# Rolling the DMA issue loop and moving 16 KB of a weight per DMA engine in a memory-bound decode kernel

## The chip, the cores and the metric

One core of one Trainium2 chip. The metric is device time in microseconds of one execution, the median of several. The kernel before takes 660.9 us. All timed runs used here are in the fast state. Four kernels (e3, e4, e7, e8) ran once each, so their state is unknown; of these the landings and packets in the trace are used, and no fine difference of their times.

## The reference

One decode step of two parallel branches whose sum is added to x: attention over a long cache (2 batches, 32 heads, 8192 cached positions of 128), and a small feed-forward part.

```python
# x: [2, 1, 512], k_cache and v_cache: [2, 32, 8192, 128], all bfloat16
xn = layernorm(x)
q = (xn @ wq) per head                       # wq: 512 x 4096
p = softmax(q . k_cache * 128 ** -0.5)
a = (p . v_cache, heads joined) @ wo         # wo: 4096 x 512
b = relu(xn @ w1) @ w2                       # w1: 512 x 1792, w2: 1792 x 512
out = x + a + b
```

The two caches are 268 of the 280.5 MB that are read; everything else is small.

## The kernel before

The 64 heads (2 batches of 32) are taken two at a time, 32 pairs in all. K and V of a pair are loads of 4 MB each, into two buffers each. SyncE issues all of the loads but that of x, unrolled over the pairs; TensorE (PE), VectorE (DVE) and ScalarE (ACT) loop. (Shortened: `out_view` stands for the output, rearranged.)

```python
sp.dma_start(w1_sb, B_w1.rearrange("(p kt) f -> p kt f", kt=KT)).then_inc(dW1, 16)
sp.dma_start(w2_sb, B_w2.rearrange("(p j) n -> p j n", j=FT)).then_inc(dW2, 16)   # FT = 14
load_k(0)
load_k(1)
load_v(0)
for t in range(NP - 2):                  # NP = 32 pairs
    sp.wait_ge(pT[NG - 1], t + 1)        # PE has transposed all of the old K
    load_k(t + R)                        # R = 2
    sp.wait_ge(sW, t + 1)                # PE has used all of the old V
    load_v(t + 1)
# ... the last V in two halves, then wo in five pieces
sp.wait_ge(sE, 1)
sp.dma_start(out_view, osb[:]).then_inc(dO, 16)
```

The feed-forward part runs before the first pair, while K is being loaded (w2 has 14 rows on each partition, so 14 matmuls):

```python
for j in range(FT):                      # PE: h = xn @ w1, 128 columns at a time
    for kt in range(KT):
        pe.matmul(hp[:, j, :], lhsT=w1_v[:, kt, j, :], rhs=xz[:, kt, Z:Z + Bsz], ...)
v.tensor_scalar(out=hT[:], in0=hp, scalar1=0.0, scalar2=None, op0=ALU.max)
for j in range(FT):                      # PE: y = relu(h) @ w2
    pe.matmul(y, lhsT=hT[:, j, :], rhs=w2_sb[:, j, :], ...)
v.tensor_tensor(out=ys[:], in0=y, in1=xsb[:], op=ALU.add)
```

At the end `ys` is put into the accumulator `fin` by four f32 matmuls against a 2x2 identity, and the products with wo are added there as the pieces of wo arrive.

## Time and profile before

| | before |
|---|---|
| median of the three runs before the prediction (of all six: 660.90) | 660.88 us |
| span of the profiled run | 658.6 us |
| data moved | 280.66 MB |
| share of the 16 DMA engines' span that the data queue fills | 99.2% |
| last piece of wo lands | 654.85 us |

The span is read first by busy shares, then by stretches, then by waits and by the end of the chain; the lines stand in the prediction below. Beside them two kinds of records of the trace are used that no view prints. One is the semaphore updates of a load: the K and V loads have 16 each, and the page counts 16 DMA engines, so I read each as one engine's landing of its share, and their 16 times show how far the engines are apart. The other is the list of the DMA packets with their size, start and duration. I give both as plain numbers.

The 16 updates of four loads of the kernel before, as microseconds after the first of them:

```
K of pair 0  (first  31.01): 0 .08 .14 .17 .19 .19 .20 .23 .24 .24 .24 .25 .26 .37 .38 | 1.72
V of pair 0  (first  50.42): 0 .10 .13 .19 .21 .22 .23 .24 .26 .27 .28 .37 .38 | 1.72 1.78 1.82
V of pair 1  (first  69.85): 0 .10 .12 .20 .21 .22 .23 .24 .35 .36 | 1.69 1.72 1.73 1.75 1.78 1.83
K of pair 31 (first 623.57): 0 .04 .14 .15 .17 .20 .21 .36 .42 | 1.69 1.71 1.73 1.74 1.76 1.82 1.84
```

Engines become late one at a time and do not catch up: one late engine at first, three by V of pair 0, six by V of pair 1, seven at the end. An engine is called late here when it stands in the right group; the differences of up to 0.4 us within a group are called start offsets.

### The profile page before, as it was taken

The numbers are of one execution on the slowest core, as the hardware profiler recorded it, in microseconds if no ns is written. First come the engines' busy times: TensorE is split into PE (matmuls) and PEld (weight loads), VectorE is DVE, ScalarE is ACT, GpSimd is POOL, SyncE is SP. The second block draws the span as 40 slices with busy tenths as digits, with TensorE's granted clock in tenths as the row PEclk, the third lists the DMA queues.
The fourth block names the chain that finished last, engine by engine and source line by source line (L and its number), as shares of the span: only waits on it lengthen the run. The fifth ranks groups of instructions, "written<-read, shape, count | busy, mean of one in ns | idle before, by whom it ended". The sixth has DMA issues, their size and how long they took to land.

```text
span 658.6 us, 26859 instructions
## 1 busy us (share of the span) xinstructions
PE 559.9 (85%) x12737; PEld 535.1 (81%) x12737; DVE 253.2 (38%) x436; ACT 255.8 (39%) x403; POOL 9.0 (1%) x46
## 2 busy tenths in 40 slices
PE   2998799987989878879887887997878997887896
PEld 0488798987879878879887887987878987887895
DVE  1144344442434433334443343443434443333441
ACT  1043444443433434334353434344333444333340
POOL 1000000000000000000000000000000000000000
PEclk9799999998998988999898899898989998898988
DMA  8999999999999999999999999999999999999996
GB/s 365 430 444 418 439 430 429 432 428 442 422 442 424 436 428 432 432 428 444 420 442 428 432 430 430 434 430 442 424 436 428 432 432 428 440 424 442 426 424 281
DMA packets 10542, 280.66 MB, mean 426 GB/s; under 512 B 1186, under 2 KB 1188, under 8 KB 1700
## 3 DMA queue, kind: packets, MB, share of 16 engines
q1 hardware_dynamic: 10528, 280.50, 99.2%
q8 instruction: 9, 0.15, 0.1%
q14 instruction: 1, 0.01, 0.0%
q10 hardware_dynamic: 4, 0.00, 0.0%
HBM read 280.50 MB, written 0.00 MB: 426 GB/s over the span
## 4 chain that ended last, share of the span: by engine, by line
DMA 58%; PE 37%; ACT 2%; issue 1%; SPq 1%; ACTq 0%; DVE 0%
DMA ks<-in_A_k_cache_dram 54%; PE tp L285 21%; PE Sc L292 11%; PE ot L305 4%; DMA w_sb<-in_A_wo_dram 4%; ACT kT L412 2%; ACT L412 1%; SPq L187 0%; PE Sc L340 0%; SPq L182 0%; PE Sc L343 0%; SPq L170 0%; SPq L169 0%; SPq L163 0%; PE ot L397 0%
## 5 line engine op out<-in xcount | busy, mean ns | idle before, releaser
L285 PE MATMUL tp<-identb,ks 128*128 128x128 bf16 x4096 | 323.5, 229 | 68.4 <-DMA ks<-in_A_k_cache_dram 68.4
L412 DVE COPY kT<-tp 128x1024 bf16<-128x1024 bf16 x320 | 219.7, 691 | 324.3 <-PE tp L285 324.2
L285 PEld LDWEIGHTS tp<-identb,ks 128*128 128x128 bf16 x4096 | 254.8, 102 | 72.3 <-DMA ks<-in_A_k_cache_dram 72.2
L412 ACT COPY kT<-tp 128x1024 bf16<-128x1024 bf16 x192 | 194.3, 1012 | 233.4 <-PE tp L285 233.3
L292 PE MATMUL Sc<-q,kT 128*128 128x64 bf16 x4096 | 216.8, 196 | 7.6 <-ACT kT L412 5.7
L292 PEld LDWEIGHTS Sc<-q,kT 128*128 128x128 bf16 x4096 | 178.4, 100 | 11.3 <-ACT kT L412 9.0
L305 PE MATMUL ot<-prm,vs 128*128 128x64 bf16 x4224 | 156.1, 192 | 4.2 <-issue 4.2
L305 PEld LDWEIGHTS ot<-prm,vs 128*128 128x128 bf16 x4224 | 139.0, 97 | 7.0 <-issue 4.4
L525 ACT COPY nm<-Sc 128x2 f32<-128x2 f32 x32 | 5.1, 160 | 118.5 <-PE Sc L343 118.5
L529 ACT ACTIVATE prm<-Sc,nm 64x128 bf16<-64x128 f32 x64 | 25.7, 401 | 4.3
L466 DVE TENSOR_REDUCE mcol<-Sc 64x1 bf16<-64x128 f32 x64 | 18.6, 290 | 18.7 <-PE Sc L292 18.3
L412 ACT ACT_TABLE_LOAD x16 | 20.5, 1283 | 2.2
L240 PE MATMUL ot<-vs,xz 128*16 128x512 bf16 x32 | 9.5, 470 | 8.6 <-DMA vs<-in_A_wq_dram 8.6
L517 ACT COPY OTf<-ot 128x2 f32 x32 | 5.1, 160 | 26.9 <-PE ot L305 26.9
L471 DVE TENSOR_REDUCE mx<-Sc 1x2 bf16<-1x128 bf16 x32 | 8.9, 278 | 16.9 <-PE Sc L340 16.9
L240 PEld LDWEIGHTS ot<-vs,xz 128*16 128x16 bf16 x32 | 3.3, 105 | 14.4 <-issue 12.2
L225 POOL COPY q<-qb 128x2 bf16<-128x2 bf16 x32 | 5.8, 184 | 588.9 <-PE Sc L292 566.1
L529 ACT ACTIVATION_READ_ACCUMULATOR prm<-Sc,nm x64 | 11.8, 185 | 0.0
L442 DVE TENSOR_SCALAR qs<-ot 16x512 bf16<-16x512 f32 x1 | 0.7, 679 | 18.0 <-PE ot L240 18.0
L340 PE MATMUL Sc<-identb,mcol 128*1 128x128 bf16 x32 | 7.0, 217 | 0.0
L270 PE MATMUL Sc<-w_sb,hT 128*2 128x512 bf16 x14 | 5.8, 604 | 0.1
L343 PE MATMUL Sc<-mx,onesb 1*128 1x2 bf16 x32 | 5.5, 172 | 0.0
(56 smaller groups left out, 37.5 us busy)
## 6 DMA issues: line engine op xcount, KB each, us to landing
ks<-in_A_k_cache_dram SPq DMA_DIRECT2D x32, 4096.0 KB, 26.7
vs<-in_A_v_cache_dram SPq DMA_DIRECT2D x31, 4096.0 KB, 31.3
vs<-in_A_wq_dram SPq DMA_DIRECT2D x1, 4096.0 KB, 12.1
vs<-in_A_v_cache_dram SPq DMA_DIRECT2D x2, 2048.0 KB, 19.3
w_sb<-in_B_w_dram SPq DMA_DIRECT2D x2, 1792.0 KB, 17.9
w_sb<-in_A_wo_dram SPq DMA_DIRECT2D x1, 1792.0 KB, 25.4
w_sb<-in_A_wo_dram SPq DMA_DIRECT2D x1, 896.0 KB, 27.1
w_sb<-in_A_wo_dram SPq DMA_DIRECT2D x1, 768.0 KB, 28.5
```

The costliest lines, as they stand in the source:

```text
L225: g.tensor_copy(q2[t % R][:], qb[:, 2 * t:2 * t + 2]).then_inc(sQ1, 1)
L240: i = pe.matmul(qp, lhsT=xz[:, kt, Z - g * Bsz:Z - g * Bsz + QG * Bsz], rhs=vs[1][:, (kt * QG + g) * 512:(kt * QG + g + 1) * 512], start=( ...
L270: i = pe.matmul(y, lhsT=hT[:, j, :], rhs=w2_sb[:, j, :], start=(j == 0), stop=(j == FT - 1),)
L285: t = pe.transpose(tp[e % 4][:, i, :], ks[r][:, kk * Dh:(kk + 1) * Dh], identb[:])
L292: t = pe.matmul(Sc[r][:, 2 * kk:2 * kk + 2 * REP], lhsT=kT[e % 4][:, i, :], rhs=rep(q2[r][:]), start=True, stop=True,)
L305: t = pe.matmul(ot[r][:, 0:2 * REP], lhsT=vs[r][:, kk * Dh:(kk + 1) * Dh], rhs=rep(prm[r][:, kk, :]), start=(kk == 0), stop=(kk == KB - 1),)
L340: pe.transpose(tr_of(r), mcol[r][:], identb[:]).then_inc(sT, 1)
L343: pe.matmul(bc_of(r), lhsT=onesb[:], rhs=mx[r][:], start=True, stop=True).then_inc(sB, 1)
L412: fn(kT[e % 4][:], tp[e % 4][:]).then_inc(kR[e], 1)
L466: m = v.tensor_reduce(out=mcol[i][half, :], in_=S_of(i)[half, :, u], axis=AX.X, op=ALU.max)
L471: v.tensor_reduce(out=mx[i][:], in_=tr_of(i).rearrange("o (u m) -> o u m", u=2), axis=AX.X, op=ALU.max, negate=True,).then_inc(sX, 1)
L529: x = a.activation(out=prm[i][half, :, u], in_=S_of(i)[half, :, u], func=ACTF.Exp, bias=nm[i][half, u:u + 1], scale=1.0, accum_out=RS[half ...
```

## The change

It has three parts. SyncE's 60 steady loads become four in a loop of 15 passes, with addresses and wait values from registers. Of w2, 12 rows stay on each of the 128 partitions; the other 256 rows go to the lower 64 partitions, four on each, by eight loads of 8 partitions, meant to run on the same eight DMA engines; so these carry 16 KB more than before and the eight others 16 KB less. And at the end `ys` is transposed instead of multiplied, kept aside, and added in the last step. The intent of the second part seems to be to even out the DMA engines; it is called the shift below, and the third part the tail. The eight are called the low engines, 0 to 7, the others the high engines, 8 to 15. The trace numbers none: in the prediction this was an assumption, and the numbers of single low engines below are names for their places on the ladder of e7 (engine 7 has one extra row there, engine 6 two, and so on).

```diff
+    FA = FT - 2
+    FB = 2 * (FT - FA)
+    FJ = FA + FB
...
-        sp.dma_start(w2_sb, B_w2.rearrange("(p j) n -> p j n", j=FT)).then_inc(dW2, 16)
+        sp.dma_start(
+            w2_sb[:, 0:FA, :], B_w2[0:P * FA, :].rearrange("(p j) n -> p j n", j=FA)
+        ).then_inc(dW2, 16)
+
+        w2_v = B_w2[P * FA:, :].rearrange("(j p) n -> p j n", p=HP)
+        for p in (0, 1, 2, 3, 32, 33, 34, 35):
+            sl = slice(p, p + 29, 4)
+            sp.dma_start(w2_sb[sl, FA:FJ, :], w2_v[sl]).then_inc(dW2b, 16)
         load_k(0)
         load_k(1)
         load_v(0)
-        for t in range(NP - 2):
-            sp.wait_ge(pT[NG - 1], t + 1)
-            load_k(t + R)
-            sp.wait_ge(sW, t + 1)
-            load_v(t + 1)
+        reg = nc.alloc_register(mybir.EngineType.SP, "pairno_sp")
+        sp.reg_mov(reg, 0)
+        with sp.Fori(0, NP // R - 1) as tr:
+            for r in range(R):
+                sp.reg_add(reg, reg, 1)
+                sp.wait_ge(pT[NG - 1], reg)
+                sp.dma_start(
+                    ks[r][:], K_all[bass.ds(tr * (R * P) + (R + r) * P, P), :]
+                ).then_inc(dK[r], 16)
+                sp.wait_ge(sW, reg)
+                sp.dma_start(
+                    vs[1 - r][:], V_all[bass.ds(tr * (R * P) + (1 + r) * P, P), :]
+                ).then_inc(dV[1 - r], 16)
...
-        for j in range(FT):
+        for j in range(FJ):
+            half = slice(0, HP if j >= FA else P)
             i = pe.matmul(
                 y,
-                lhsT=hT[:, j, :],
-                rhs=w2_sb[:, j, :],
+                lhsT=hT[half, j, :],
+                rhs=w2_sb[half, j, :],
...
-            pe.matmul(
-                fin[:, k, :],
-                lhsT=ys[:, k * P:(k + 1) * P],
-                rhs=ident2[:],
-                start=(k == 0),
-                stop=False,
-            )
+            t = pe.transpose(yst[:, k, :], ys[:, k * P:(k + 1) * P], ident2[:])
+        t.then_inc(sH, 1)
...
-        v.tensor_scalar(
-            out=hT[:], in0=hp, scalar1=0.0, scalar2=None, op0=ALU.max,
-        ).then_inc(sF, 1)
+        for o, h in (
+            (hT[:, 0:FA, :], hp[:, 0:FA, :]),
+            (hT[0:HP, FA:FJ:2, :], hp[0:HP, FA:FT, :]),
+            (hT[0:HP, FA + 1:FJ:2, :], hp[HP:P, FA:FT, :]),
+        ):
+            t = v.tensor_scalar(out=o, in0=h, scalar1=0.0, scalar2=None, op0=ALU.max)
+        t.then_inc(sF, 1)
...
-        v.tensor_copy(yT[:], ot[0][:, 0:KT * Bsz].rearrange("p (b c) -> p b c", c=KT)).then_inc(sV, 1)
+        v.tensor_tensor(
+            out=yT[:],
+            in0=ot[0][:, 0:KT * Bsz].rearrange("p (b c) -> p b c", c=KT),
+            in1=xT[:].rearrange("p c b -> p b c"),
+            op=ALU.add,
+        ).then_inc(sV, 1)
```

(Cut: buffer sizes, the new semaphore, the w1 columns that go with the rows, and the counts of later waits.)

More of the change, by code (lines that the diff above doesn't have):

```diff
@@ L72 @@
     vs = [sb([P, SLOT], bf16, f"vs{i}") for i in range(R)]
-    w_sb = sb([P, max(WJ * D, KT * Dff + FT * D)], bf16, "w_sb")
+    w_sb = sb([P, max(WJ * D, KT * Dff + FJ * D)], bf16, "w_sb")
     w1_sb = w_sb[:, 0:KT * Dff].rearrange("p (kt f) -> p kt f", kt=KT)
-    w2_sb = w_sb[:, KT * Dff:KT * Dff + FT * D].rearrange("p (j n) -> p j n", j=FT)
+    w2_sb = w_sb[:, KT * Dff:KT * Dff + FJ * D].rearrange("p (j n) -> p j n", j=FJ)
     wo_sb = w_sb[:, 0:WJ * D].rearrange("p (j n) -> p j n", j=WJ)
@@ L106 @@
     OX = sb([P, WJ, Bsz], bf16, "OX")
-    hT = sb([P, FT, Bsz], bf16, "hT")
+    hT = sb([P, FJ, Bsz], bf16, "hT")
     ys = sb([Bsz, D], f32, "ys")
+    xT = sb([P, KT, Bsz], f32, "xT")
     yT = sb([P, Bsz, KT], bf16, "yT")
@@ L123, in bc_of @@
         return Sc[i][:, 480:482]
-    dX, dO, dW1, dW2 = sem("dX"), sem("dO"), sem("dW1"), sem("dW2")
+    dX, dO, dW1 = sem("dX"), sem("dO"), sem("dW1")
+    dW2, dW2b = sem("dW2"), sem("dW2b")
     dK = [sem(f"dK{i}") for i in range(R)]
@@ L153 @@
     y = Sc[1][0:Bsz, :]
+    yst = ot[0][:, 16:16 + KT * Bsz].rearrange("p (c b) -> p c b", c=KT)
     fin = ot[0][:, 0:KT * Bsz].rearrange("p (b c) -> p c b", c=KT)
@@ L248, in _ @@
         pe.wait_ge(dW1, 16)
-        w1_v = w1_sb.rearrange("p kt (f j) -> p kt j f", j=FT)
+        w1_a = w1_sb[:, :, 0:P * FA].rearrange("p kt (f j) -> p kt j f", j=FA)
         for j in range(FT):
@@ L254, in _ @@
                     hp[:, j, :],
-                    lhsT=w1_v[:, kt, j, :],
+                    lhsT=w1_a[:, kt, j, :] if j < FA else w1_sb[:, kt, j * P:(j + 1) * P],
                     rhs=xz[:, kt, Z:Z + Bsz],
@@ L268, in _ @@
         pe.wait_ge(dW2, 16)
-        for j in range(FT):
+        pe.wait_ge(dW2b, 16 * 8)
+        for j in range(FJ):
+            half = slice(0, HP if j >= FA else P)
             i = pe.matmul(
                 y,
-                lhsT=hT[:, j, :],
-                rhs=w2_sb[:, j, :],
+                lhsT=hT[half, j, :],
+                rhs=w2_sb[half, j, :],
                 start=(j == 0),
-                stop=(j == FT - 1),
+                stop=(j == FJ - 1),
             )
@@ L400, in _ @@
                         rhs=OX[:, j, :],
-                        start=False,
+                        start=(j == 0 and k == 0),
                         stop=(j == WJ - 1 and k == KT - 1),
@@ L490, in _ @@
         ).then_inc(sV, 1)
+        v.wait_ge(sH, 2)
+        v.tensor_copy(xT[:], yst)
         v.wait_ge(sW, NP + 1)
@@ L494, in _ @@
         ).then_inc(sV, 1)
-        v.wait_ge(sH, 2)
+        v.wait_ge(sH, 3)
         v.tensor_copy(Ob[:], tp[0][0:H, 0:Bsz, :]).then_inc(sV, 1)
-        v.wait_ge(sH, 3)
+        v.wait_ge(sH, 4)
         v.tensor_copy(
@@ L500, in _ @@
         ).then_inc(sV, 1)
-        v.wait_ge(sH, 4)
-        v.tensor_copy(yT[:], ot[0][:, 0:KT * Bsz].rearrange("p (b c) -> p b c", c=KT)).then_inc(sV, 1)
         v.wait_ge(sH, 5)
+        v.tensor_tensor(
[4 more added lines that the diff above has]
+        ).then_inc(sV, 1)
+        v.wait_ge(sH, 6)
         v.tensor_copy(osb[:], tp[1][0:Bsz * KT, 0, :]).then_inc(sE, 1)
```

## The prediction

> **What bounds the kernel now.** I read the page first: busy shares, slices and DMA queues.
>
> ```profile
> span 658.6 us, 26859 instructions
> PE 559.9 (85%) x12737; PEld 535.1 (81%) x12737; DVE 253.2 (38%) x436; ACT 255.8 (39%) x403; POOL 9.0 (1%) x46
> DMA  8999999999999999999999999999999999999996
> ...
> DMA packets 10542, 280.66 MB, mean 426 GB/s; under 512 B 1186, under 2 KB 1188, under 8 KB 1700
> ...
> q1 hardware_dynamic: 10528, 280.50, 99.2%
> q8 instruction: 9, 0.15, 0.1%
> ```
>
> No compute engine is full, and the 16 DMA engines are: the data queue q1 alone fills 99.2% of their span. Then the same by stretches (microseconds from the start; columns are length, then PE, PEld, DVE, ACT and POOL busy, granted clock, DMA share, GB/s):
>
> ```profile
> 0.00:33.00 33.00, 19.51 (x114) 8.94 (x115) 4.05 (x13) 2.94 (x4) 3.43 (x16) 0.90 0.95 398
> 150.00:600.00 450.00, 388.15 (x8971) 378.84 (x8968) 179.92 (x304) 182.26 (x288) 4.42 (x24) 0.94 1.00 432
> 600.00:640.00 40.00, 34.10 (x776) 33.49 (x773) 15.50 (x27) 15.88 (x25) 0.00 (x0) 0.91 1.00 429
> 640.00:658.60 18.60, 13.18 (x356) 11.94 (x353) 2.05 (x8) 1.23 (x6) 0.00 (x0) 0.85 0.73 303
> ```
>
> For 450 us the share is 1.00 at 432 GB/s: there is no hole to fill. Next, who waits: first the kernel's engines, then the DMA-issuing queue of SyncE.
>
> ```profile
> PE tp L285 <- DMA ks<-in_A_k_cache_dram: 68.4, 27, 3.4
> ```
>
> ```profile
> SPq L158 <- PE tp L285: 429.8, 30, 39.8
> SPq L161 <- PE ot L305: 148.6, 30, 8.2
> ```
>
> PE waits for K tiles 27 times; SyncE mostly sleeps until a buffer comes free, and is never short of time. Last, the end of the chain (start, length, what):
>
> ```profile
> 625.69 0.04 issue
> 625.73 29.12 DMA w_sb<-in_A_wo_dram
> 654.85 0.05 issue
> 654.90 0.39 PE ot L397 x8
> 655.29 0.02 issue
> 655.31 0.18 DVE yT L502
> 655.49 0.04 issue
> 655.53 0.28 PE tp L406
> 655.81 0.02 issue
> 655.84 0.21 DVE osb L504
> ```
>
> The last piece of wo lands at 654.85 and 3.8 us of small work follow. So the end is set by the moment at which the slowest DMA engine finishes its share of the queue.
>
> The trace's semaphore updates refine this, since each load posts one update per DMA engine. For K tile 0 (issued at 2.36) 15 updates come between 31.01 and 31.39 and one at 32.73. The number of late ones grows to seven by 110 us and stays: for the last K tile nine come at +0.00 to +0.42 us and seven at +1.69 to +1.84. The group means are 0.19 and 1.76, 1.57 apart. The last wo piece has eight early and eight late. The nine 16384-byte packets of q8 start at 29.57, 41.77, 47.79, 54.95, 61.06, 68.32, 107.20, 650.36 and 654.27: seven by 110, one more before the end, one after most data. So one instruction fetch makes one engine about 1.57 us late, for good, because its queue never runs dry. At the first fetch that is seen directly: the fetch holds an engine for 1.06 us and that engine's next 32 KB takes 1.681 instead of 1.213. The other engines' 32 KB packets stay at 1.213 meanwhile, so the limit is each engine's own rate (27 GB/s), not a shared one.
>
> [...] Against a fear of loops, PE, DVE and ACT already loop 16 times here and only one fetch falls between 70 and 650 us. [...] The trace gives no engine numbers; it shows 16 updates per load.
>
> **The change, part by part.**
>
> *w2.* Before, w2 is 14 rows of 1 KB on each partition; an engine has 8 packets of 14336 bytes, 535 ns each: 4.28 us. After, every partition takes 12 rows. A 12288-byte packet, interpolated between the 7168-byte (274) and 16384-byte (615) packets, is about 463 ns, so 8 take 3.70: minus 0.58 us on all engines. The other 256 rows go by eight loads of 8 partitions[...], to engines 0 to 7: 32 packets of 1 KB for each of these. The two 1 KB packets of x took 44 ns, so 1.41 us, plus seven more semaphore writes at 9 ns: 1.47. Net: engines 8 to 15 have 0.58 us less, engines 0 to 7 have 0.9 us more. Bytes are the same in total.
>
> This pays if the fetches sit on engines 8 to 15. I take that as the author's reason for picking the low engines; no number in the trace proves it. Then late engines, at most +1.84 now, come to about +1.26, and the early ones, at most +0.42, to about +1.32. The maximum falls from 1.84 to 1.32: **0.52 us off the last landing**, and off the time.
>
> *Rolled SyncE.* Sixty unrolled loads become four in a loop of 15 passes. Issues take 0.33 us each before[...]. A K load is issued 26.7 us before it lands and needs about 9.7 us of service (4.19 MB at 432 GB/s), so 17 us of lateness would be hidden. The shorter program may save a fetch[...] and seven late engines instead of eight leave the last one where it is. Effect: 0.
>
> *Start.* Eight more issues at about 0.46 us delay K tile 0's issue from 2.36 to about 6, with data queued until beyond 21 us: 0. The second feed-forward product has 16 matmuls instead of 14 at 0.43 (+0.85), the relu three small operations instead of one of 0.19 (about +0.35). It ended at 32.4, just before K tile 0 landed; now at about 33.6. PE begins its pairs about 1 us late, the load of K tile 2 is issued at 44.7 instead of 43.7, and V tile 0 keeps the engines busy to 50.4: 5.7 us of slack, so 0.
>
> *Tail.* Four f32 transposes replace matmuls that took 1.05 us at 643.59. They are off the path: PE has OX at 650.1 and then waits for wo. The copy of x for the later addition waits beside other work. The final yT gains an addend: 0.17 us becomes about 0.19. Effect: +0.02.
>
> Sum: 660.88 - 0.52 + 0.02 = **660.4 us**.
>
> **The rivals.** First, the fetches sit on low engines, or are spread over both halves. Then a low engine is at +1.84 + 0.9 = +2.74, and the time is 660.88 + 0.9 = 661.8. For it: the trace has no engine numbers. Against: the change would be senseless, and its 16 KB each way (0.6 us down, 0.9 up) splits a 1.57 us gap almost in half, which looks designed. I give it one in six.
>
> Second, the 1 KB packets cost much more than 44 ns each under load, say 70: then low engines gain 1.7 and the end is +2.1, 661.2. For it: 44 ns was seen on idle engines. Against: 2048-byte packets took 85 ns under full load, the same per byte.
>
> Third, the DMA limit is shared, so moving bytes between engines gives nothing: 660.9. Against: the constant 1.213 us beside the stalled engine.
>
> Fourth, the SyncE loop itself fetches at its branches, 15 times: spread over 8 engines, up to two each, 3 us more, 664. Against: the three loops that are there already do not.
>
> **Range and chances.** Runs of before spread over 0.2 us. The main case (about seven in ten) gives 660.0 to 660.8; rivals two and three end just above; so 659.9 to 661.3 should hold it 8 times in 10. A change of 2% is 13.2 us and nothing here is that large: within 2% 0.985, faster 0.005, slower 0.01.
>
> **What would show it.** Right: the last semaphore updates of steady K loads spread about 1.3 us instead of 1.84, with the groups nearly merged; DMA share still 1.00 at 432 GB/s from 150 to 600 us; q8 with eight or nine packets; PE's first transposes after 33 us without moving later landings; the last wo piece at about 654.3. Wrong: a spread above 2 us (fetches on low engines or dear small packets), many more q8 packets (the loop fetches), or DMA share below 1.00 in the middle (SyncE late).

The sum came to 660.88 - 0.52 + 0.02 = 660.38, given as 660.4. In the changed kernel's loop a register instruction took 53 ns in front of a K load, median of 30. The 0.02 for the tail is my estimate, which names no number behind it; for scale, two-input DVE operations at the end of the kernel before took 0.16 us (128x2) and 0.22 (128x62).

## The result, and the profile after

The changed kernel takes 661.47 us (six runs, 661.33 to 661.53) against 660.90 (six runs, 660.83 to 661.04): 0.57 us slower, with no overlap, and just outside the stated range of 659.9 to 661.3. A ratio is the mean time of one kernel's runs over that of the other's of the same rounds, so not quite the ratio of these medians: here 1.0008, with a 95% interval of 0.9995 to 1.0021. By the 2% measure it is the same; what follows is about half a microsecond, far inside that interval, and rests on medians, on ranges of runs and above all on landing times.

The page of the changed kernel, the parts on busy shares, slices and queues:

```profile
span 659.3 us, 27035 instructions
PE 556.7 (84%) x12735; PEld 533.9 (81%) x12735; DVE 253.6 (38%) x439; ACT 255.9 (39%) x403; POOL 8.9 (1%) x46
DMA  8999999999999999999999999999999999999996
...
DMA packets 10862, 280.66 MB, mean 426 GB/s; under 512 B 1250, under 2 KB 1508, under 8 KB 2020
...
q1 hardware_dynamic: 10848, 280.50, 99.1%
q8 instruction: 9, 0.15, 0.1%
```

The bytes are the same and the queue is as full; there are 320 more packets (256 of 1 KB and 64 semaphore writes). The nine fetches (the 16 KB packets on queue q8, which the page calls instruction) are still nine, so the shorter SyncE program saved none. By stretches, columns as before:

```profile
0.00:33.00 33.00, 17.09 (x124) 8.56 (x125) 4.33 (x15) 2.94 (x5) 3.29 (x16) 1.00 0.97 404
150.00:600.00 450.00, 388.24 (x8962) 379.27 (x8958) 180.02 (x302) 183.94 (x289) 4.29 (x23) 0.94 1.00 432
```

The middle is the same to the last digit of GB/s: the loop on SyncE does not starve the queue. The waits of SyncE's queue and of PE:

```profile
SPq L194 <- PE tp L309: 414.1, 30, 29.8
SPq L198 <- PE ot L329: 142.8, 30, 8.0
```

```profile
PE tp L309 <- DMA ks<-in_A_k_cache_dram: 70.0, 27, 3.4
```

SyncE still sleeps 557 us and PE still waits for K 27 times. The end of the chain:

```profile
626.89 28.59 DMA w_sb<-in_A_wo_dram
655.48 0.05 issue
655.53 0.39 PE ot L416 x8
655.92 0.02 issue
655.94 0.18 DVE yT L527
656.12 0.04 issue
656.16 0.28 PE tp L425
656.45 0.02 issue
656.47 0.21 DVE osb L534
```

From landing to the last copy it takes 1.20 us, as before (654.85 to 656.05); yT with its addition takes 0.18, not more. The last landing alone has moved, from 654.85 to 655.48, by 0.63. The landing times show where that comes from. The last K load, as microseconds after its first update:

```
before (first 623.57): 0 .04 .14 .15 .17 .20 .21 .36 .42 | 1.69 1.71 1.73 1.74 1.76 1.82 1.84
after  (first 623.02): 0 .05 .14 | 1.43 1.45 1.51 1.54 1.57 1.62 1.64 1.66 1.67 1.73 1.85 | 2.82 3.07
```

Two groups have become three, of 3, 11 and 2 engines. This is what would arise if five of the seven fetches until then fell on high engines and two on low ones: three high engines without a fetch; six low engines with the extra rows and five high ones with a fetch; and two low engines that carry both. The first engine is 0.55 us earlier than before, the last 0.68 us later (626.09 against 625.41).

### The profile page after: what moved, and what is told of

It is laid out like the page before. It is cut to its first block, busy times and chain, and to the rows that moved or that the text cites. A ratio compares the mean times of both kernels' runs of the same rounds, so it can differ in the third digit from the quotient of the medians.

```text
span 659.3 us, 27035 instructions
## 1 busy us (share of the span) xinstructions
PE 556.7 (84%) x12735; PEld 533.9 (81%) x12735; DVE 253.6 (38%) x439; ACT 255.9 (39%) x403; POOL 8.9 (1%) x46
## 3 DMA queue, kind: packets, MB, share of 16 engines
q1 hardware_dynamic: 10848, 280.50, 99.1%
## 4 chain that ended last, share of the span: by engine, by line
DMA 57%; PE 37%; ACT 2%; SPq 2%; issue 2%; ACTq 0%; DVE 0%
DMA ks<-in_A_k_cache_dram 53%; PE tp L309 21%; PE Sc L316 11%; PE ot L329 4%; DMA w_sb<-in_A_wo_dram 4%; ACT kT L431 2%; SPq L184 1%; ACT L431 1%; SPq L209 0%; PE Sc L364 0%; SPq L194 0%; SPq L204 0%; PE Sc L367 0%; SPq L177 0%; SPq L176 0%
## 5 line engine op out<-in xcount | busy, mean ns | idle before, releaser
L416 PE MATMUL ot<-OX,w_sb 128*128 128x2 bf16 x128 | 4.1, 166 | 2.9 <-DMA w_sb<-in_A_wo_dram 2.8
L416 PEld LDWEIGHTS ot<-OX,w_sb 128*128 128x128 bf16 x128 | 3.7, 100 | 3.3 <-DMA w_sb<-in_A_wo_dram 2.2
```

The lines of the kernel that those rows point to most:

```text
L416: t = pe.matmul(fin[:, k, :], lhsT=wo_sb[:, j, k * P:(k + 1) * P], rhs=OX[:, j, :], start=(j == 0 and k == 0), stop=(j == WJ - 1 and k == ...
```

## The experiments

Sixteen runs; e13 repeats the changed kernel and e14 repeats e9. The table has the timed ones. They were made each on one chip with the kernel before beside it (five executions of a run, nine of the kernel before); "over before" is the difference of the medians. "Lands" is the last update of wo in the profiled run.

| run | what differs from before | median | before | over before | lands |
|---|---|---|---|---|---|
| e1 | SyncE's loop alone | 660.85 | 660.87 | -0.02 | 654.99 |
| e5 | the tail alone | 660.74 | 660.91 | -0.17 | 654.91 |
| e2 | shift and tail, no loop | 661.63 | 660.87 | +0.76 | 655.84 |
| e13 | the changed kernel again | 661.70 | 660.88 | +0.82 | 655.80 |
| e9 | half the shift (with loop and tail) | 661.50 | 660.89 | +0.61 | 655.58 |
| e14 | the same again | 661.32 | 660.88 | +0.44 | 655.53 |
| e15 | half the shift by four small loads | 661.08 | 660.88 | +0.20 | 655.08 |
| e16 | eight tiny loads, nothing moved | 661.55 | 660.88 | +0.67 | 655.62 |
| e6 | twice the shift | 662.48 | 660.91 | +1.57 | 656.38 |
| e10 | rows to engines 0 to 4 (loop, tail) | 660.69 | 660.89 | -0.20 | 655.01 |
| e11 | rows to engines 0 to 4 alone | 660.65 | 660.89 | -0.24 | 655.01 |
| e12 | rows to engines 0 to 4, and the tail | 660.56 | 660.89 | -0.33 | 654.76 |

In all of them, and in the first profiles of both kernels, the time of the profiled run is the last landing of wo plus 5.83 to 5.98 us. So what the change does to the time is what it does to the slowest DMA engine. Of the twelve, only e6 has an interval of the ratio clear of 1 (1.0009 to 1.0036). The kernel before was profiled once (654.85, in a run of 660.69, just under its six others), so a landing is compared with it only to about 0.2 us.

### e1_roll_only and e2_w2_and_tail: which part costs it

```diff
# e1: the kernel before, with only
-        for t in range(NP - 2):
...
+        with sp.Fori(0, NP // R - 1) as tr:
...
# e2: the changed kernel, with only this turned back
```

> The kernel before with SyncE's loop alone. Theory A (the 16 KB shift of w2 hits DMA engines that already carry an instruction fetch, and the loop is innocent): the same as before within 0.15 us, steady K landings spread 1.8 us with nine early and seven late engines, nine fetch packets. Theory B (the loop or its register-addressed loads cost the time): +0.5 to +0.6 us over before, nothing changed in the spread or more fetch packets.

> The changed kernel with SyncE unrolled again (w2 split and the new tail stay). Theory A: +0.5 to +0.6 us over before as the changed kernel has, steady landings spread 3.1 us in three groups of about 3, 11 and 2 engines. Theory B: no slower than before, and by the prediction even 0.5 us faster.

The loop alone: 660.85 against 660.87, nine fetches, nine early and seven late engines. Without the loop the changed kernel is at 661.63 with its three groups (last K: three at 0 to 0.39 us, eleven to 2.58, two at 3.30 and 3.48; the one at 2.58 seems to be the high engine that stood at 1.01 in K of pair 0, 0.57 above the rest of its group, before it had a fetch). That is 0.76 over before, a little more than the 0.5 to 0.6 expected. The loop is innocent; the shift or the tail costs the time. The queues of e1 show that it saved no fetch:

```profile
q1 hardware_dynamic: 10528, 280.50, 99.1%
q8 instruction: 9, 0.15, 0.1%
```

### e5_tail_only: the tail, or the shift

```diff
# the kernel before, with
+            t = pe.transpose(yst[:, k, :], ys[:, k * P:(k + 1) * P], ident2[:])
# in place of the matmuls on ident2, and yT = fin + xT at the end
```

> The kernel before with the new tail alone (four f32 transposes and a later addition in place of the matmuls on ys); w2 and SyncE as before. Theory A (the 16 KB shift of w2 costs the time): within 0.15 us of before. Rival C (the tail costs it, since the first call has not told the two apart): +0.5 to +0.7 us.

660.74 (660.67 to 660.86) against 660.91 (660.76 to 661.21). The tail does not cost it. Whether it gains 0.17 us is not settled: the ranges overlap, and the profiled run's last landing (654.91) is not earlier.

### e3_ladder_before and e4_ladder_after: which engines the fetches fall on, first try

```diff
+        at = 0
+        for k in range(2, 16):
+            sp.dma_start(lad[at:at + k, :], A_wo_rows[at:at + k, :]).then_inc(dL, 16)
+            at += k
         load_k(0)
```

(The rows are 16 KB each, taken from the K cache. Every engine was meant to carry one row more than the next; at 0.615 us a row in the kernel before, fourteen make 8.6 us, the longest step. No run shows such an order for more than eight engines.)

> The kernel before with 14 extra loads of 16 KB rows[...]. About 8 to 10 us slower by the longest ladder step. Theory A: the seven fetches before 110 us show as seven engines that each jump by 1.57 us, some of them among engines 0 to 7. Theory of the prediction: all of them among engines 8 to 15.

> The changed kernel with the same ladder. Theory A: engines 0 to 7 sit 1.48 us higher than in the ladder on before; exactly two of the fetches up to 110 us (the fourth and the fifth, at about 54 and 61 us) fall on them and five on engines 8 to 15. If the placement is fixed by the program and not by chance, the same engines as in the ladder on before. Rival: the engines differ between the two ladders, so the placement is not to be relied on.

678.60 and 679.72, twice the slowdown expected, and useless for their purpose. The 119 packets of the ladder in e3 took 1.276 us on average where a 16 KB packet takes 0.615 elsewhere. I had put the k rows of a load on k neighbouring partitions; in the next pair of runs, where the rows were spread over every fourth partition, the packets took 0.611 (e7) and 0.620 (e8). Why the neighbouring ones took longer is not shown. In my reading, for which I give no landings, the engines at the bottom then ran dry and lost the lead by which they were to be recognized.

### e7_low_ladder_before and e8_low_ladder_after: the same for the low half

```diff
+        for k, p in zip(range(2, 9), (0, 1, 2, 3, 32, 33, 34)):
+            sl = slice(p, p + 4 * k - 3, 4)
+            sp.dma_start(lad[sl, :], lad_v[sl, :]).then_inc(dL, 16)
         load_k(0)
```

> The kernel before with seven extra loads of 16 KB rows, for the k lowest engines with k = 2 to 8[...]: engine 7 gets 0.62 us more, engine 6 1.24, and so on to 4.3 us for engines 1 and 0; engines 8 to 15 stay at the bottom. Theory A: five of the fetches until 110 us lift an engine at the bottom by 1.57 us, and two, the fourth and the fifth, lift an engine of the ladder. Rival: all seven lift engines at the bottom here, and it was the changed program that moved two of them.

> The changed kernel with the same low ladder, engines 0 to 7 another 1.48 us higher. Theory A: again five fetches at the bottom and two on the ladder, on the same two engines as in the kernel before, so that the placement belongs to the fetch's number and not to chance.

This ladder is meant to give each low engine a load of its own: engine 7 one extra row, engine 6 two, and so on to seven for engines 1 and 0, so that the landing order tells the low engines apart. The high engines are to get none and stand at the bottom, that is, land first. The queue of e7 has 70 packets more than before (10598 against 10528), the 35 rows and a semaphore write for each. The trace of e7 (663.44 us), landings after the first, with fetches at 29.68, 45.40, 52.30, 59.41 and 66.01:

```
V of pair 0 (first 50.53): 0 .05 .09 .16 .21 .26 | .76 1.25 1.71 1.72 1.86 2.28 3.35 3.83 4.38 4.46
K of pair 2 (first 61.01): 0 .02 .05 .13 .26 .40 .54 1.05 1.16 1.63 1.84 2.60 2.74 3.07 3.61 3.71
V of pair 1 (first 70.71): 0 .01 .05 .09 .28 .42 1.04 1.14 1.65 1.85 2.09 2.60 2.76 3.05 3.62 3.71
```

In the first line the bottom group has six members and two fetched ones at 1.71 and 1.72; the ladder reads 0.76 (engine 7), 1.25 (6), 1.86 (5), 2.28 (4), 3.35, 3.83, 4.38 and 4.46: eight engines near the one to seven steps of 0.62 that were meant. Before the next line the bottom engines ran dry for 0.77 us (10.48 us between first landings, where a tile takes 9.71), so every other lead shrinks by about 0.72. Engine 5 should then stand at 1.14 and there should be three engines with a fetch near 1.0, 1.0 and 1.8; but the line has one entry more at 2.74 and one less near 1.14. So the fourth fetch lifted engine 5, by 1.6. In the third line 0.54, which is engine 6, has gone and 2.09 has come: the fifth fetch lifted engine 6, by 1.55. The first three, and the next two, each took one from the bottom.

e8 (665.14 us) gives the same pair. Before K of pair 2 its bottom ran dry for 2.3 us, by which engine 5 falls from 3.56 to 1.25 and engine 6 from 2.92 to 0.60; the line of K has no 1.25 but 2.76, and the line after it no 0.60 but 2.12. So in both kernels fetches four and five fall on engines 5 and 6. In the eight low engines no other hit is seen until the end; so the others go to engines 8 to 15, by elimination. One engine up or down would be possible from the ladder alone, since neighbouring steps differ by 0.6 us and start offsets by up to 0.4.

### e6_double_shift: twice the dose

```diff
-    FA = FT - 2
+    FA = FT - 4
```

> The changed kernel with twice the shift: 10 rows of w2 on every partition, 8 by the lowest engines. Theory A: the low engines with a fetch, which already end last, get another 0.88 us (32 packets of 1 KB at 46 ns, less 0.59), so about 662.4 us, 1.5 over before, and the steady landings spread 4.5 us. A theory in which the small packets cost nothing, or in which the shift works as the prediction had it, gives no such slope; rival C gives no change against the changed kernel, 661.5.

662.48, 1.57 over before, where 1.5 was expected; the spread is 4.27 where 4.5 was. The trace is the clearest of all (K of pair 31 has the same pattern as this V of pair 1, except for the seventh fetch):

```
V of pair 0 (first 49.65): 0 .02 .05 .13 .32 | 1.72 1.76 1.95 | 2.61 2.63 2.67 2.68 2.72 2.77 2.95 3.01
V of pair 1 (first 69.11): 0 .01 .11 .17 .27 | 1.67 1.71 1.76 | 2.55 2.58 2.62 2.65 2.91 2.96 | 4.15 4.28
```

Three fetches on high engines by about 50 us, and then the fourth and the fifth on two of the eight loaded ones. The end of its chain follows the two:

```profile
627.38 29.00 DMA w_sb<-in_A_wo_dram
...
656.43 0.39 PE ot L416 x8
```

### e9_half_shift, e14_half_again, e13_after_again, e15_half_four_loads, e16_eight_tiny_loads: the size of the cost

```diff
# e9, e14: the changed kernel with
-    FA = FT - 2
+    FA = FT - 1
# e15: besides this, four rows on 32 partitions instead of two on 64
-        for p in (0, 1, 2, 3, 32, 33, 34, 35):
+        for p in (0, 1, 2, 3):
# e16: the kernel before with eight more loads into a spare buffer
+        for p in (0, 1, 2, 3, 32, 33, 34, 35):
+            sl = slice(p, p + 29, 4)
+            sp.dma_start(lad[sl, :], B_w2[sl, :]).then_inc(dL, 16)
```

(e13 is the changed kernel without an edit. Cut from e15 and e16: the counts, slices and the spare buffer that follow from what is shown.)

> The changed kernel with half the shift: 13 rows of w2 on every partition, 128 rows to engines 0 to 7. All engines lose 0.29 us, the eight low ones get 16 packets of 1 KB (0.74) back. Theory A: engines 5 and 6, which carry a fetch, end about 0.44 us later than without a shift; since the latest without a shift is 0.1 to 0.2 us above them, 0.2 to 0.4 us over before, 661.1 to 661.3.

> The changed kernel once more, on the chip of the next three: 661.4 to 661.6 as before, 0.5 to 0.7 over before.

> The half shift once more. If its 661.50 was chance (start offsets of the DMA engines differ by some tenths from run to run): 661.1 to 661.3. If it is real, so that half the rows cost as much as all: 661.5 again.

> The half shift by four small loads (8 partitions of 4 rows each) instead of eight (8 partitions of 2 rows), on partitions 0 to 31. The same bytes on the same engines. If a part of the cost belongs to the number of small loads and not to the bytes: 0.1 to 0.3 us less than the half shift by eight. If only bytes count: the same as it within 0.05.

> The kernel before, w2 whole as before, and eight extra loads of 8 rows of 1 KB for engines 0 to 7[...]: 8 packets and 8 semaphore writes more on each low engine (about 0.38 us), nothing less on the others. Theory A: engines 5 and 6 end 0.38 us later, 0.1 to 0.3 over before, 661.0 to 661.2. If eight small loads by themselves cost the half microsecond, whatever they carry: 661.4 or more.

e9 missed: 661.50, as slow as the whole shift, where 661.1 to 661.3 was expected. Repeated beside the whole shift on one chip, half was 661.32 (661.11 to 661.39) and the whole 661.70 (661.45 to 661.74), so a part of the miss was scatter. (The repeats are not quite where they were expected either: e13 is 0.82 over before instead of 0.5 to 0.7, and e14 just above the 661.1 to 661.3 that was named for chance.) The other part seems to belong to the number of small loads. e15 has the bytes of e14 on the same engines in four loads instead of eight and is at 661.08, 0.24 us under it by the median, though their ranges touch (661.06 to 661.20 and 661.11 to 661.39). And e16, which carries only 8 KB more on each low engine and takes nothing off any, is at 661.55, where bytes alone gave 661.0 to 661.2; it is the 661.4 or more that was named for small loads that cost by themselves.

The packets account for it. In all of these runs a 1 KB packet starts 42 ns or so after the one before it on its engine, a semaphore write takes about 6 more. In e16 that makes 8 times 48 ns, 0.38 us on each low engine, as expected. But after them, of the first 32 packets of K of pair 0 on the 16 engines, fourteen take 1.28 to 1.50 us where all 32 take 1.213 in the kernel before; the excess sums to 3.0 us, on average 0.38 for each of the eight low engines. The same sum is 0.11 in e9, 0.03 in the changed kernel and 0 in e15. It is large where each small load gives an engine one row, small with two, gone with four rows in four loads. In e6 (eight rows each) it is 0.04 on each low engine, while the first packets of the eight high engines, which run beside the small ones, take 1.30 to 1.83 us, an excess of 0.38 on each that does not reach the end of the chain. Why these packets are longer is not shown; the sums are.

With this, the extra time of a low engine and the measured slowdown go together:

| run | 1 KB packets, semaphore writes | taken off | longer packets | low engine's extra | over before |
|---|---|---|---|---|---|
| e15 | 16 x 0.042 + 4 x 0.006 = 0.70 | 0.30 | 0 | 0.40 | 0.20 |
| e9, e14 | 16 x 0.042 + 8 x 0.006 = 0.72 | 0.30 | 0.11 | 0.53 | 0.61, 0.44 |
| e16 | 8 x 0.042 + 8 x 0.006 = 0.38 | 0 | 0.38 | 0.76 | 0.67 |
| changed, e2, e13 | 32 x 0.042 + 8 x 0.006 = 1.39 | 0.60 | 0.03 | 0.82 | 0.57, 0.76, 0.82 |
| e6 | 64 x 0.042 + 8 x 0.006 = 2.74 | 1.20 | 0.04 | 1.58 | 1.57 |

"Taken off" is eight of the larger w2 packets: 535 ns with 14 rows, 498 with 13, 460 with 12, 385 with 10. The last column is up to 0.25 below the one before it (and once 0.08 above). A likely reason, not tested: without a shift the end is set by the worst start offset among all engines with a fetch, and with it by two engines only. The scatter of 0.1 to 0.2 us between calls is of the same size.

### e10_five_lowest, e11_five_plain, e12_five_tail: the shift, aimed

If engines 5 and 6 are the trouble, rows for engines 0 to 4 alone should help. 120 rows lie on partitions 0 to 19, six rows each; each of four loads takes every fourth partition, five in all, as the ladder's load of five rows did, and so is expected on engines 0 to 4. The last 8 rows are one load of 8 partitions. The queue of e12 has 56 packets more than before (10584 against 10528): 28 for these rows and 28 semaphore writes, five for each of the four loads and eight for the last. That the five are engines 0 to 4 was not read from a trace; it rests on the ladder and on the times below.

```diff
# on the kernel before (e11), with the new tail (e12), on the changed kernel (e10)
+    FA = FT - 1
+    FJ = FA + 7
+    rows = [P] * FA + [20] * 6 + [8]
...
+        w2_v = B_w2[P * FA:P * FA + 120, :].rearrange("(p j) n -> p j n", j=6)
+        for p in range(4):
+            sl = slice(p, p + 17, 4)
+            sp.dma_start(w2_sb[sl, FA:FA + 6, :], w2_v[sl]).then_inc(dW2b, 16)
+        sp.dma_start(w2_sb[0:8, FA + 6, :], B_w2[P * FA + 120:, :]).then_inc(dW2b, 16)
...
-                lhsT=hT[:, j, :],
-                rhs=w2_sb[:, j, :],
+                lhsT=hT[0:rows[j], j, :],
+                rhs=w2_sb[0:rows[j], j, :],
```

> The changed kernel with the same 128 rows, but 120 of them for engines 0 to 4 alone (no fetch falls on these by the ladders), in 4 packets of 6 KB each on 20 partitions[...]; the last 8 rows for engines 0 to 7. Theory A with the placement from the ladders (fetches 4 and 5 on engines 5 and 6): every engine with a fetch ends 0.25 to 0.29 us earlier, engines 0 to 4 about 0.7 us later, still before them; so 0.2 to 0.3 us under before, 660.6. If the placement is wrong by an engine and one of 0 to 4 has a fetch: 661.5 or more. [...]

> The kernel before with these 120 rows for engines 0 to 4 and nothing else of the change. Theory A: the same 0.2 to 0.3 us under before, as SyncE's loop and the tail are innocent.

> The kernel before with the rows for engines 0 to 4 and the new tail, SyncE unrolled. Theory A: 0.3 to 0.4 us under before, if the 0.17 us that the tail alone showed is real, else 0.2 to 0.3.

660.69, 660.65 and 660.56 against 660.89: by the medians the sign has turned, by 0.20, 0.24 and 0.33 us, where the same number of rows (e9) had cost 0.61. The number of small loads does not explain this: e15 has four of them and is 0.20 over before, these have five and are below it. Without one run in each that stands 1.0 to 1.5 us above the median (before has two, by 0.8 and 0.9, among nine), e12 has 660.48 to 660.60 and before 660.74 to 661.21; the ranges of e10 and e11 overlap with it. The end of e12's chain:

```profile
626.24 28.52 DMA w_sb<-in_A_wo_dram
...
654.81 0.39 PE ot L412 x8
```

The last landing is 654.76, the earliest of all profiled runs. In e10 and e11 it is 655.01, later than the 654.85 of the kernel before; their profiled runs were slow among their own (660.85 and 660.84), so here the gain rests on the medians and is not seen in a landing. e12 beats both kernels by the median, the one before by 0.33 us and, across calls, the changed one by 0.9; as a ratio it is 0.9998 with an interval of 0.9984 to 1.0011, so it is no more than the end of an argument.

## Why the prediction was wrong, point by point

- **What bounds the kernel** was right: the slowest DMA engine's last landing plus a constant. The constant was 5.83 to 5.98 us in all 14 profiled runs that the table and the result name.
- **One fetch makes one engine 1.57 us late for good** was right. The steps of 1.55 and 1.6 in e7 and the groups of e6 show it.
- **The step that failed** is "This pays if the fetches sit on engines 8 to 15. I take that as the author's reason for picking the low engines". Two of the eight that matter sit on engines 5 and 6 (e7, e8), so the latest engine became later instead of earlier: the spread of the last K load went from 1.84 to 3.07 and not to about 1.3, and the last landing moved by +0.63 us and not by -0.52. The prediction had this as its first rival, at one in six; the trace held no evidence for the assumption, and trust in the author's intent was given the weight of evidence.
- **The size in that rival** was too large: it gave 661.8, measured are 661.47 to 661.70 in three sets of runs with the shift whole. The low engine's extra was 0.82 instead of 0.9, because 1 KB packets in a row start 42 ns apart, not 44, and the semaphore writes add 6 ns, not 9. The rest may be that the two engines do not have the worst start offset, which the rival took for them: the last K load's last update is 0.68 us later than before.
- **The second rival**, dear small packets, was not the cause, but small loads are dearer than their packets in one respect that it did not have: the packets after eight one-row loads are longer (e16).
- **The third rival**, a shared limit, falls: with the bytes the same in total, moving rows changes the end, by 1.57 us in e6; e12 goes the other way, but only by the medians.
- **SyncE's loop costs nothing** was right (e1), and so was that it saves no fetch that matters: nine on q8 in both kernels. So the fourth rival, fetches at its branches, which nothing in the trace had suggested, did not happen.
- **The start** was right in effect, wrong in detail: the eight small loads took 0.73 us each to issue, so K of pair 0 was issued at 8.42 us and not at about 6, which did no harm since its first packet started at 20.43. The feed-forward part ended earlier, not later, in the changed kernel's profile (30.55 against 33.06 us, its matmuls 0.22 us apart instead of 0.42), with a granted clock from 23 to 33 us of 1.00 against 0.66. This differs between runs and not between kernels: in e13, the same program, they were 0.40 apart on average, at 0.66. The load of K of pair 2 was issued at 43.46, no later than before (43.72), and in e13 at 44.15; 44.7 was forecast.
- **The tail** was right: yT takes 0.18 us.
- **Of the signs to look for**, the spread above 2 us had been named for the case of fetches on low engines. It came: 3.07.

What stays open: why fetches four and five go to engines 5 and 6 and the others to the upper half, and whether another program or chip has the same assignment; why packets after very short loads are longer; and whether the tail gains a tenth.

## What to carry to other kernels

Here the DMA engines were full from start to end (the data queue filled 99.2% of their span before, 99.1% after), the time was the slowest engine's last landing plus 5.83 to 5.98 us, and the spread of a load's 16 semaphore updates told how many engines were late and by how much (seven, by 1.57 us). Evening engines out by hand needs the identity of the late ones: put a known extra load on a known subset, and see which group the late ones join, before bytes are moved. Two late engines on the wrong side turned a forecast gain of 0.52 us into a loss of 0.57, and the most that there was to gain was about half a microsecond in 661.
